# One transfer per tail, a new written order, and q of one batch transposed by DMA

## The chip, the cores and the metric

The kernel runs on one core of a Trainium2 chip. The metric is device time in microseconds (us), as the median of the timed runs. The core has a matrix engine (PE; its weight loads are listed as PEld), a vector engine (DVE), an activation engine (ACT), a general engine (POOL) and a sync engine (SP), which here issues every DMA from one queue in order (SPq is its sequencer).

## The reference

Two blocks follow one another. The first is attention with pooled keys: q, k and v are (8 batches, 8 heads, 576 tokens, 64). k and v are averaged over groups of 8 tokens, so each head has 72 pooled keys and values, and

```python
scores = scale * np.matmul(q, k_p.transpose(0, 1, 3, 2))
attn = softmax(scores)
x = matmul(attn, v_p)            # (8, 8, 576, 64), then reshaped to (8, 576, 512)
```

The second is a mixture of four attention experts on x. A gate picks two of four experts for each token, with softmax weights w. Each expert projects x to q, k and v of 64 columns, does causal attention over the 576 tokens, and projects back to 512 columns with wo. The output, (8, 576, 512) in float32, is the sum of the two picked experts, weighted by w.

## The kernel before, in words

**Tiles.** A batch's 576 tokens are handled as 512 main tokens, in four chunks of 128, and 64 tail tokens. The tails of two batches (an even one and the odd one after it) are put together to 128 rows and go through a path of their own (`part_t`, run with the odd batch).

**Units.** The work is cut into named units such as `3:s2` (batch 3, scores of head pair 2). A unit is a Python generator: its first step mostly issues the PE work, the next steps copy the result out of PSUM on DVE or ACT, mask on POOL, or store. The string `ORDER` at the top lists every step of every unit, and the loop at the end of the kernel issues them in just that order; each engine keeps it (`keep_in_program_order`). So the order of every engine's queue, and of SP's DMAs, is written out by hand in `ORDER`. A wait at the head of a queue holds everything behind it.

The names that matter here, by batch `b`:

- `lq`, `lk`, `lv` load the main tokens of q, k, v as float32 (batch 0 in four pieces, batch 1 in two); `lqt`, `lkt`, `lvt` load the tails. `W:lq`, `W:lk`, `W:lv`, `W:lo` load the weights, `W:c0` to `W:c3`, `W:cv`, `W:co` cast them.
- `qc` casts q to bf16 (`qbf`), `ks` and `vs` add up pairs of tokens, `kt` and `vt` cast the tails of k and v.
- `q0` to `q3` transpose q, one head pair each: four PE transposes into `qT_ps`, then a DVE copy to `qT`.
- `kp` and `vp` pool k and v by matmuls with the mask tiles `pm` (main) and `pmt` (tail).
- `s0` to `s3`: scores into `sA_ps`, then the exponential on ACT into `etA`. `a0` to `a3`: times v into `oA_ps`, then normalised on DVE into `x_tm`.
- `x0` to `x3`: transposes of x on PE; in batches 6 and 7 the DMA queue does them (`xd0` to `xd3`).
- `p0` to `p3`, `v0`, `v2`: projections into `p_ps` and `v_ps`; `g1` to `g6`: the gate; `c..`: expert scores (`sB_ps`, `etB`, `etC`); `o0`, `o1`: expert attention times values (`oB_ps`); `t0`, `t1`: its transposes (by DMA in batches 4, 5, 6); `w`, `y`, `z`: the output projection (`y_ps`), its copy (`w` on ACT, `y` on DVE, `z` both) and the store.
- `qt`, `qx`, `sx`, `ax`, `xx`, `pt`, `vx`, `h0`, `h1`, `hd`, `ox`, `tx`, `w4`: the same for the tails of two batches. `w4` ends with `yt_ps`, a copy to `ofin` and the store; `7:w4` is the last unit of the kernel.
- `W:h0` to `W:h31`: fillers, two matmuls each of zeros into `idle_ps`, 31 of them ahead of the first projection and one near the end.

**What is allotted.** PSUM is shared by two pools: `ps1` (two tiles) and `ps2` (three). The raw float32 tiles have two buffers for each of q, k and v, `ofin` has four. Each DMA signals on one of eight semaphores in turn, and waits until the DMA eight places ahead of it has landed.

**q in the last batches.** q's row r of a group of four neighbouring tokens lies in `qbf[:, r]`. In batches 0 to 5 the transposes of r write runs of 32 elements into `qT_ps`, with gaps between them, and the copy is plain. In batches 6 and 7, whose x the DMA queue transposes, tokens must stand in their natural order; there the transposes write without gaps and the copy (`COPY_IN_ORDER`) puts tokens in order.

**Tails of k and v.** A tail is loaded by two DMAs: heads 0 to 3 into partitions 0 to 63, heads 4 to 7 into partitions 64 to 127. `pmt[0]` and `pmt[1]` are the pooling masks of the two halves.

Of the kernel before, what the change touches and what calls it, by code (L numbers as in the profile page):

```python
# [22 lines left out]
0:lk2 0:qc2a 1:q0 1:q1 0:qc0a W:h29 0:qc0d 1:q1 W:h1 0:lk0 W:h21 0:qc1d 0:qc1a 0:lk3 0:q0 0:lv0 W:h7
W:h3 0:qc3d 0:q0 0:ks2 0:q1 0:lk1 0:q1 0:lv2 W:h8 0:ks3 W:h19 W:h14 0:kp2 0:lvt 0:qc2d 0:lv3 0:ks0
0:q2 0:kp2 0:lv1 0:q2 1:kt W:h6 0:vs2 1:lq1 W:h2 0:kp3 0:ks1 W:h27 0:qc3a W:h18 0:q3 1:lk0 0:kp3
0:q3 0:kp1 0:s2 0:vs0 1:lk1 0:kp1 0:s1 0:vs3 0:vt 0:vs1 0:s3 0:kp0 W:h26 0:kp0 1:lv1 W:h15 0:vp 0:s1
0:s2 1:lvt W:h25 0:vp 1:lv0 W:h22 1:qc1a 0:s3 0:a2 1:qc1d 0:s0 W:h16 W:lk W:h24 0:a3 W:h5 0:lqt 0:a2
1:q2 1:ks0 W:h13 1:ks1 1:kp0 0:a3 1:q2 0:s0 0:a1 1:kp0 0:a0 W:h4 1:kp1 W:h28 1:q3 0:a0 1:kp1 0:a1
W:h17 1:s0 0:x0 1:s0 1:s2 1:q3 1:s3 0:x0 1:s1 W:lq W:lv 1:s2 1:lqt 1:vs1 0:x1 1:s3 2:lq W:h10 W:h9
0:x3 0:x1 1:vt W:h0 W:c1 0:x2 1:vs0 2:lkt 0:x3 2:lk W:c3 0:x2 1:vp 1:vp 0:p1 1:a0 1:a2 1:a2 1:s1  # L30
0:p1 W:c2 W:c0 0:p3 1:a1 1:qt 1:a0 2:qc 2:lv 1:a1 0:p3 0:p2 1:a3 W:cv 0:p0 0:p2 0:v2 0:p0 1:a3 2:kt
3:lqt 1:x2 0:v2 1:qx 0:c10 0:c10 0:c2 0:v0 2:lvt 1:qx 1:x3 1:x2 0:v0 0:c2 1:x0 1:x3 3:lk 0:c11 1:x0
1:sx 1:x1 1:x1 0:c11 0:c11 0:c00 0:c00 0:g1 0:g2 2:q3 2:q3 2:q0 1:sx 1:v2 0:c2 3:lvt 2:q2 0:c01 2:ks
2:lqt 0:c10 3:lkt 1:ax 2:q2 2:q1 2:q0 1:ax 1:p1 1:p1 1:v0 0:c01 2:kp 2:q1 1:v2 1:p2 2:vs 2:kp 0:g3
2:vt 1:v0 1:xx 2:s2 3:lq 1:xx 1:p2 2:s0 2:s1 1:vx 0:g4 2:s2 2:s1 1:vx 2:s0 3:lv 1:g1 2:s3 0:g5 1:g2
2:vp 0:o1 2:vp 2:s3 1:pt 2:a2 0:g6 3:ks 1:pt 3:kt 2:a0 1:p3 4:lq 3:qt 0:c01 0:o1 2:a3 2:a2 0:c00
1:p0 1:g3 2:a0 1:p3 2:a3 2:a1 1:c11 3:qc 3:kp 1:p0 4:lk 3:qx 3:vt 2:a1 1:hd 3:qx 1:c11 1:h0 1:hd
1:c2 3:kp 2:x2 2:x1 1:h0 2:x2 4:lkt 0:o0 2:x1 2:x3 4:lv 4:lvt 2:x0 1:c10 1:c2 1:g4 0:o0 3:sx 2:x3
1:c00 3:q1 2:x0 1:c2 1:c10 1:c00 3:q3 1:h1 3:q1 3:q3 3:q2 3:q0 2:v2 3:vs 1:h1 3:q2 1:c11 4:qc 3:q0
5:lq 0:t0 1:g5 0:t1 2:v0 2:v2 3:sx 3:s3 3:s1 0:t1 3:vp 0:t0 3:s3 2:p1 6:lvt 1:hd 4:ks 3:s1 2:p1 2:v0  # L40
3:s2 4:kt 1:c10 3:s0 3:vp 3:s2 3:a3 2:p0 3:a3 4:q2 3:a1 3:ax 4:q2 3:s0 4:q1 1:c01 2:p0 4:q3 4:q1
2:p3 1:c01 2:p3 5:lqt 2:c01 3:a1 4:q3 4:q0 3:ax 2:c01 3:a0 1:c00 4:q0 4:kp 4:kp 3:a2 3:a0 3:a2 2:p2
3:xx 2:p2 6:lkt 1:g6 4:s2 3:xx 4:s0 4:s0 5:lkt 4:s2 1:ox 3:x3 2:g1 1:c01 4:vt 1:o0 2:c00 4:s1 1:ox
3:x3 3:x1 4:vs 2:g2 2:c00 5:qc 4:vp 3:x1 4:s1 3:pt 4:s3 2:c11 3:pt 4:vp 1:o0 3:x0 3:x2 1:o1 2:c01
3:x0 W:lo 3:x2 5:q2 4:lqt 4:s3 2:c00 5:lk 2:c11 3:p3 5:q2 5:lvt 5:q3 1:o1 5:lv 2:c2 3:p3 2:c10 5:q1
4:a3 5:kt 2:c2 5:q3 2:c10 3:p1 4:a0 5:q1 3:p1 W:co 4:a3 3:p2 3:vx 4:a0 6:lqt 4:a1 3:p2 3:vx 3:v0
4:a1 7:lqt 3:v0 0:w0 2:g3 3:hd 6:lq 3:c10 2:c11 1:t1 4:a2 5:qt 2:g4 5:ks 0:w0 3:p0 1:t1 5:q0 4:a2
3:c10 3:hd 5:q0 5:vt 3:p0 3:h0 2:c2 3:c11 5:qx 5:kp 3:c11 3:v2 5:kp 5:qx 2:g5 0:w3 3:v2 3:h0 2:g6
4:x1 4:x1 5:s3 0:w3 3:g1 5:s1 4:x2 5:vs 1:t0 7:lkt 5:s3 2:c10 2:o0 6:lk 4:x2 0:w2 1:t0 4:x0 6:qc
2:o0 5:sx 5:s1 3:c2 3:c10 6:vt 0:w2 5:sx 5:s0 5:s0 7:kt 6:lv 3:c11 3:g2 4:x0 4:x3 5:vp 4:x3 3:c2  # L50
5:vp 3:hd 2:o1 4:p1 3:c2 2:o1 0:w1 4:p1 6:kt 5:s2 3:h1 0:w1 6:q3 6:q0 5:ax 6:q3 4:p0 6:q0 2:t0 3:h1
6:ks 5:ax 5:s2 3:g3 2:t0 0:w3 7:lvt 4:v2 2:t1 4:p0 6:q1 5:a2 3:g4 2:t1 7:qt 6:vs 5:a0 6:q1 5:a0 1:w3
4:p3 5:a1 1:w3 4:p3 5:a2 4:v2 4:p2 7:lq 5:xx 3:c00 3:c01 4:p2 5:a1 0:w2 6:kp 5:a3 3:c00 7:lk 5:xx
3:c01 6:kp 3:g5 3:g6 7:ks 0:w0 5:pt 6:q2 6:s3 5:a3 4:c01 6:q2 4:c00 5:pt 1:tx 1:tx 6:vp 5:x0 6:s3
4:v0 4:c00 5:x0 6:vp 2:w1 4:c01 4:v0 5:x3 6:s0 4:c2 2:w1 5:x1 5:x3 6:s1 5:x1 0:w1 6:s0 7:qc 6:s1
7:lv 2:w0 5:x2 3:o1 6:a0 5:x2 3:c01 2:w0 1:w4 3:c00 3:o1 5:p3 1:w4 4:c2 7:kp 6:a0 7:kp 4:g1 4:c10
4:c11 6:s2 5:p3 7:vs 4:c11 4:c10 7:q3 1:w4 3:ox 6:s2 7:q3 7:q2 5:v0 4:c10 3:ox 2:w1 6:a3 5:vx 7:q2
5:v0 2:w2 5:vx 6:a2 6:a1 6:a3 6:a2 1:w0 2:w2 1:w0 4:g2 2:w0 5:p2 2:w3 5:p2 5:hd 7:s3 6:a1 1:w0 7:q1
2:w3 5:hd 7:q1 4:c00 7:vt 4:c2 5:hd 5:v2 4:c11 4:g3 1:w2 3:t1 5:h1 7:s3 7:s1 1:w2 5:h1 7:s1 6:xd2
5:v2 2:w3 3:t1 7:vp 5:g1 5:p1 6:xd3 7:s2 4:g4 2:w2 7:vp 5:c10 5:p1 7:a3 7:s2 7:a3 7:q0 7:q0 4:g5  # L60
5:p0 3:o0 5:g2 4:c01 3:o0 7:qx 6:xd0 5:p0 4:o0 1:w1 5:c10 5:c2 7:s0 4:g6 7:qx 6:xd1 1:w1 3:t0 7:s0
6:p3 5:g3 3:t0 3:tx 3:tx 6:v2 6:p3 6:p0 5:c2 7:a1 1:w1 4:o0 7:a0 3:w4 6:v2 4:t0 7:a1 6:p0 1:w2 3:w4
6:p1 7:a2 5:g4 7:a0 3:w2 3:w2 5:h0 7:a2 5:c10 5:g5 7:sx 4:o1 6:p1 4:o1 1:w3 3:y1 3:y1 6:p2 5:c11
7:sx 5:h0 5:g6 5:c01 7:xd0 7:xd1 5:c11 6:p2 5:c01 5:c00 5:ox 6:v0 4:t1 3:w2 3:w3 5:ox 3:w3 3:w0 6:v0
3:w0 5:c01 7:ax 7:v0 7:ax 7:v0 4:w2 5:c11 7:xx 7:xd3 6:c2 5:c2 7:xx 6:g1 5:c00 3:y1 4:w2 6:c00 5:o1
4:w3 6:c2 7:xd2 5:o1 7:vx 3:w3 7:v2 3:w4 6:g2 6:c2 4:w3 7:p2 6:c11 6:c00 6:c10 6:g3 5:c00 7:v2 7:p2
6:c11 7:vx 6:c01 5:t1 7:p3 4:y1 6:g4 7:p3 4:w3 7:g1 4:y1 6:c10 4:y1 5:o0 5:o0 7:g2 6:c01 6:c00 6:g5
4:y0 4:y0 5:t0 7:p0 6:c11 6:c10 6:o1 7:c11 7:p0 6:g6 7:c10 6:c01 7:g3 7:g4 6:o1 4:w2 7:p1 5:tx 6:o0
5:tx 6:o0 7:c10 7:p1 7:c10 3:w0 7:c11 5:w4 5:y1 6:t1 7:g5 7:c2 7:c01 5:w4 7:c2 7:c00 7:c11 5:y1 4:y0
7:g6 5:y2 7:c01 7:pt 7:c2 7:c01 7:pt 5:y2 6:t0 7:c00 5:y1 5:y0 5:y0 7:c00 7:o1 5:w3 7:o1 7:hd 6:y1  # L70
# [919 lines left out]
```

## Time and profile before

| | |
|---|---|
| median of the timed runs | 178.21 us (3 runs, 177.66 to 178.53) |
| the profiled execution | 176.43 us |
| its span | 174.7 us |
| granted TensorE clock, mean | 0.996 |
| HBM read, written | 30.42 MB, 9.44 MB |

The profile shows one execution. Its span runs from the first to the last instruction; the execution's own time is a little longer. Instructions are listed by the tile that they write and read (`qT_ps<-ident,qbf`), since all stand on one line of a helper. Matmuls overlap one another, so their durations don't add up to PE's time: what a further one costs is read from the length of a group of them. "Idle before" an instruction names the one whose end released it.

### The profile page before, as it was taken

What the parts mean: (1) busy time and instruction counts of PE and PEld (TensorE: products, weight loads), DVE (VectorE), ACT (ScalarE), POOL (GpSimd) and SP (SyncE); (2) the same over time, 40 slices, a digit from 0 to 9 for tenths busy, and PEclk for the clock granted to TensorE, in tenths of its full rate; (3) what the DMA queues carried; (4) which work ended last, traced back from release to release, by engine and by line L of the source; (5) the groups of instructions that cost most, each with busy time, mean ns of one, the idle gap of its engine ahead of it and who ended that gap; (6) DMA issues with size and microseconds to landing.
All of it is one profiled execution on the core that took longest, in us unless ns stands there. A gap on an engine that the chain in (4) does not pass through costs nothing.

```text
span 174.7 us, 5295 instructions
## 1 busy us (share of the span) xinstructions
PE 163.1 (93%) x2088; PEld 101.2 (58%) x2088; DVE 123.7 (71%) x354; ACT 125.0 (72%) x176; POOL 101.2 (58%) x227
## 2 busy tenths in 40 slices
...
GB/s 151 280 337 304 344 296 282 263 325 262 250 221 345 346 281 288 190 209 311 260 284 339 332 365 365 25 177 67 172 72 90 183 181 157 90 135 250 267 332 194
DMA packets 52968, 42.03 MB, mean 241 GB/s; under 512 B 21968, under 2 KB 48080, under 8 KB 52944
## 3 DMA queue, kind: packets, MB, share of 16 engines
...
HBM read 30.42 MB, written 9.44 MB: 228 GB/s over the span
## 4 chain that ended last, share of the span: by engine, by line
PE 72%; DMA 11%; ACT 8%; DVE 4%; SPq 1%; issue 1%; ACTq 0%; DVEq 0%
PE p_ps L133 15%; PE v_ps L133 7%; PE y_ps L133 6%; PE idle_ps L133 5%; PE sB_ps L133 5%; PE sA_ps L133 4%; PE oA_ps L133 4%; PE qT_ps L133 4%; PE oB_ps L133 4%; PE vp_ps L133 3%; DMA out_dram<-ofin 3%; DMA ktail<-in_k_dram 3%; PE xT_ps L133 3%; DMA kraw<-in_k_dram 3%; PE oBt_ps L133 3%; ACT etA L133 3%
## 5 line engine op out<-in xcount | busy, mean ns | idle before, releaser
L133 ACT ACTIVATE etA<-sA_ps 72x1024 bf16<-72x1024 f32 x32 | 31.4, 1018 | 12.7 <-PE sA_ps L133 12.6
L133 ACT ACTIVATE etB<-sB_ps 128x1024 bf16<-128x1024 f32 x32 | 32.3, 1027 | 3.0 <-PE sB_ps L133 2.7
L133 PE MATMUL p_ps<-xT,wqk 128*128 128x512 bf16 x128 | 32.9, 379 | 0.1
L133 POOL TENSOR_SCALAR_AFFINE_SELECT etB<-etB 128x256 bf16<-128x256 bf16 x48 | 18.5, 407 | 12.0 <-ACT etB L133 11.8
L133 ACT CAST qk<-p_ps 128x512 bf16<-128x512 f32 x32 | 18.8, 587 | 9.2 <-PE p_ps L133 9.0
L133 DVE TENSOR_TENSOR x_tm<-oA_ps,rzA 128x512 bf16<-128x512 f32 x32 | 22.1, 691 | 1.1
L133 POOL TENSOR_TENSOR vsum<-vraw 128x512 bf16<-128x512 f32 (+2 forms) x18 | 18.4, 1043 | 7.5 <-DMA vraw<-in_v_dram 7.5
L133 PE MATMUL idle_ps<-idle 128*128 128x512 bf16 x64 | 19.6, 418 | 1.9 <-DVE idle L160 1.2
L133 PEld LDWEIGHTS <-wqk 128*128 128x128 bf16 x192 | 15.0, 97 | 10.3 <-issue 0.9
L133 POOL TENSOR_TENSOR ksum<-kraw 128x512 bf16<-128x512 f32 (+1 forms) x16 | 17.8, 1134 | 4.8 <-DMA kraw<-in_k_dram 4.6
L133 PE MATMUL y_ps<-wo_t,oT 128*128 128x512 bf16 x64 | 18.4, 379 | 1.0 <-DMA oT<-o_sc 0.7
L133 DVE COPY qT<-qT_ps 128x512 bf16<-128x512 bf16 x32 | 15.2, 486 | 5.8 <-PE qT_ps L133 5.5
L133 ACT COPY ofin<-y_ps 128x512 f32<-128x512 f32 x20 | 11.7, 586 | 10.0 <-PE y_ps L133 6.8
L133 PE MATMUL v_ps<-wvg,xT 128*128 128x260 bf16 x128 | 17.0, 274 | 0.0
L133 PE MATMUL qT_ps<-ident,qbf 128*128 128x128 bf16 x128 | 11.9, 220 | 2.1 <-DVE qbf L133 1.4
L133 PE MATMUL sB_ps<-qk 64*128 64x256 bf16 (+3 forms) x128 | 13.6, 299 | 0.0
L133 DVE COPY xT<-xT_ps 128x512 bf16<-128x512 bf16 x24 | 9.7, 419 | 4.6 <-PE xT_ps L133 4.5
L133 PEld LDWEIGHTS <-xT 128*128 128x128 bf16 x128 | 11.6, 97 | 2.4 <-DVE x_tt L133 0.4
L133 POOL CAST qbf<-qraw 128x2048 bf16<-128x2048 f32 x6 | 11.3, 1889 | 2.8 <-PE sB_ps L133 2.4
L133 PEld LDWEIGHTS <-etA 72*128 72x128 bf16 x256 | 10.6, 97 | 3.9 <-issue 1.0
L133 PEld LDWEIGHTS <-qbf 128*128 128x128 bf16 x128 | 8.3, 97 | 7.4 <-issue 2.7
L133 PEld LDWEIGHTS <-etB 128*128 128x128 bf16 x256 | 11.4, 97 | 1.7 <-POOL etB L133 0.5
...
## 6 DMA issues: line engine op xcount, KB each, us to landing
out_dram<-ofin SPq DMA_DIRECT2D x28, 256.0 KB, 2.7
...
qraw<-in_q_dram SPq DMA_DIRECT2D x4, 256.0 KB, 4.7
...
kraw<-in_k_dram SPq DMA_DIRECT2D x4, 256.0 KB, 4.8
```

The source lines that it names most:

```text
L133: return tc.keep_in_program_order(fn(*args, **kwargs))
```

## The change

1. **Tails of k and v.** One DMA loads a tail. Partition 2t + half then holds token t, heads 0 to 3 (half 0) or 4 to 7 (half 1). The masks `pmt` are made anew: one mask over pairs of partitions on POOL, multiplied on DVE by the parity of the partition.
2. **Stores of tails.** `w4` stores the tails of both batches by one DMA. In `7:w4` the copy to `ofin` is split: the first 256 columns on ACT, the others on DVE.
3. **q of batch 7.** Four DMA transposes (`7:qd0` to `7:qd3`), one for each r, write `qT`; the units `7:q0` to `7:q3`, with 16 PE transposes and four DVE copies, are gone. The transposed tile keeps its four r apart, and the scores matmul of batch 7 reads it so and writes each result to the place of its token: every fourth float32 of `sA_ps`.
4. **Order.** `ORDER` is written anew throughout.

The diff without `ORDER`, of which three places follow:

```diff
+Q_BY_DMA = (7,)
-COPY_IN_ORDER = (6, 7)
+COPY_IN_ORDER = (6,)
+SCORES_IN_ORDER = (7,)
...
     pm = pooling("pm", 0, POOLW // NR)
-    pmt = [pooling("pmt0", MAIN, POOLW), pooling("pmt1", MAIN - 64, POOLW)]
-    nc.gpsimd.memset(pmt[1][0:64, :], 0.0)
+    rows = pooling("pmr", 2 * MAIN, 2 * POOLW)
+    parity = const.tile([128, 2, 1], BF16, name="parity")
+    nc.vector.tensor_reduce(
+        out=parity[:, :, 0], in_=ident[:, :].rearrange("p (i half) -> p half i", half=2),
+        axis=AX_X, op=MAXOP,
+    )
+    pmt = []
+    for half in range(2):
+        t = const.tile([128, 128], BF16, name=f"pmt{half}")
+        nc.vector.tensor_tensor(
+            out=t[:], in0=rows[:], in1=parity[:, half, :].to_broadcast([128, 128]), op=MULT
+        )
+        pmt.append(t)
...
-            for half in range(2):
-                sp.dma_start(
-                    out=t[half * 64 : half * 64 + 64, :].rearrange("p (h d) -> p h d", h=4),
-                    in_=srcs[nm][b, half * 4 : half * 4 + 4, MAIN:S, :].rearrange("h t d -> t h d"),
-                )
+            sp.dma_start(
+                out=t[:].rearrange("p (h d) -> p h d", h=4),
+                in_=srcs[nm][b, :, MAIN:S, :].rearrange("h t d -> t h d"),
+            )
...
+        def q_dma(r):
+            if "qD" not in st:
+                st["qD"] = apool.tile([128, NR, NHP, 128], BF16, name="qT", tag="qT")
+            sp.dma_start_transpose(
+                out=st["qD"][:, r, :, :], in_=st["q"][:, r, :, :].rearrange("p h d -> p (h d)")
+            )
...
+                to, rhs = ps[:, hh, :], st["qT"][r0 : r0 + D, hp, :] if "qT" in st else None
+                if b in SCORES_IN_ORDER:
+                    to = to.rearrange("s (p r) -> s r p", r=NR)
+                    rhs = (
+                        st["qD"][r0 : r0 + D, :, hp, :] if "qD" in st
+                        else rhs.rearrange("d (r p) -> d r p", r=NR)
+                    )
                 pe.matmul(
-                    out=ps[:, hh, :], lhsT=kp[r0 : r0 + D, hp, :],
-                    rhs=st["qT"][r0 : r0 + D, hp, :], start=True, stop=True,
+                    out=to, lhsT=kp[r0 : r0 + D, hp, :], rhs=rhs, start=True, stop=True,
                 )
...
+        if b in Q_BY_DMA:
+            names.update({f"qd{r}": lambda r=r: q_dma(r) for r in range(NR)})
...
             t = ofp.tile([128, DM], FP32, name="ofin", tag="ofin")
-            copy(out=t[:], in_=ps[:])
-            yield
-            for i, b_ in enumerate(both):
-                store(out[b_, MAIN:S, :], t[i * TAIL : (i + 1) * TAIL, :])
+            if b < B - 1:
+                copy(out=t[:], in_=ps[:])
+            else:
+                for half, eng in ((slice(0, DM // 2), act.copy), (slice(DM // 2, DM), dve.tensor_copy)):
+                    eng(out=t[:, half], in_=ps[:, half])
+            yield
+            store(out[b - 1 : b + 1, MAIN:S, :], t[:])
```

Of the order: the head of the list, before and after, and the place of the transposes of q in the new list, up to the first scores that need them.

```diff
-0:lq0 W:h12 1:lq0 0:lkt W:h20 0:lq2 0:lq3 W:h30 0:kt 1:qc0a W:h23 1:lkt W:h11 1:qc0d 0:lq1 1:q0
+W:h21 W:h1 0:lq0 0:lk0 0:qc0d 0:lq3 W:h24 W:h15 0:qc3a 0:lq1 W:h18 0:qc0a 0:qc1d 0:lkt W:h2 W:h14
...
+4:c01 2:w1 5:x1 3:c01 5:x1 6:s0 2:w1 6:s1 6:s0 7:lv 1:tx 5:x0 4:c2 1:tx 5:x2 3:g5 7:qd0 6:s1 5:x0
+5:x2 6:a3 7:ks 2:w0 0:w1 7:qd2 5:p3 3:g6 3:o1 4:c2 7:qd1 2:w1 6:s2 3:c00 6:a3 2:w0 4:c11 5:vx 4:c01
+4:g1 3:o1 5:p3 7:qd3 7:kp 4:c10 6:s2 4:c11 4:c10 4:c2 5:hd 5:vx 3:ox 7:qt 2:w0 7:kp 5:hd 6:a1 1:w4
+1:w4 6:a0 3:ox 4:g2 6:a2 6:a1 4:g3 6:a2 1:w4 7:vs 1:w0 6:a0 5:hd 1:w0 4:g4 2:w3 5:v2 2:w2 2:w3 2:w2
+5:p2 5:p2 7:s3 2:w3 5:v2 5:h1 7:s2 7:s3 7:vp 7:vp 1:w2 5:h1 5:v0 1:w2 5:p1 7:qx 7:s2 4:c11 5:v0 0:w3
...
```

More of the change, by code (lines that the diff above doesn't have):

```diff
@@ L21 @@
 ORDER = """
-0:lq0 W:h12 1:lq0 0:lkt W:h20 0:lq2 0:lq3 W:h30 0:kt 1:qc0a W:h23 1:lkt W:h11 1:qc0d 0:lq1 1:q0
[L23 to L70, printed above, removed]
@@ L71 @@
-7:o0 5:w3 6:w0 5:y2 5:y0 6:y1 7:hd 7:o0 7:h1 7:t1 6:w0 7:h0 7:t0 7:t1 7:t0 7:h1 7:hd 5:w3 5:w4 6:y3
-6:w0 6:y1 6:y3 6:y3 7:h0 7:z2 7:ox 6:w2 7:z2 7:z0 7:ox 7:tx 6:w2 7:tx 6:w2 W:h31 7:w4 7:z0 7:w4 7:w4
+W:h21 W:h1 0:lq0 0:lk0 0:qc0d 0:lq3 W:h24 W:h15 0:qc3a 0:lq1 W:h18 0:qc0a 0:qc1d 0:lkt W:h2 W:h14
+0:lk1 0:kt W:h30 W:h11 0:lq2 0:ks0 0:qc2a 1:lq1 0:lv2 0:lk3 W:h12 W:h9 0:kp0 0:lv1 0:lk2 W:h3 0:kp0
+0:qc2d 0:qc1a 0:lv0 W:h29 0:lvt 0:lv3 0:q0 W:h17 W:h13 0:qc3d 0:q0 1:lq0 0:ks1 0:q1 W:h10 1:lkt
@@ new lines @@
+W:h28 W:h26 1:lk1 0:ks3 1:lk0 0:vs0 1:lv1 0:q1 W:h5 0:vt 0:q3 0:q2 0:vs1 0:q2 0:kp1 0:q3 0:vs2 1:lv0
+0:s0 0:kp1 0:s1 0:ks2 1:ks1 1:kt W:h19 0:kp3 0:kp3 W:h4 0:kp2 1:qc1a 0:vs3 1:qc1d 1:ks0 1:lqt 0:s1
+0:vp 0:kp2 W:h23 0:s3 1:qc0d 1:qc0a 1:vs0 W:h20 1:q3 0:vp W:lq 1:lvt 1:q0 0:s0 W:lk 0:s2 0:lqt 1:vt
+1:q0 0:s3 1:q3 W:lv 0:a3 0:a1 2:lq 0:a1 W:h6 1:q2 W:h25 1:q2 0:s2 1:kp1 0:a2 W:h0 1:q1 0:a3 0:a0
+1:kp1 1:q1 0:a2 0:a0 W:h8 1:kp0 1:kp0 W:h7 1:s3 1:s3 0:x2 1:s2 1:s0 W:h22 1:vs1 2:lkt 2:lvt 2:lk
+1:s2 0:x3 0:x3 1:qt 1:s1 2:qc W:c0 1:s1 W:c2 0:x1 1:s0 0:x2 W:h16 0:x1 W:h27 0:x0 1:vp 0:x0 1:vp
@@ new lines @@
+W:c1 0:p2 1:a3 2:kt 0:p0 W:c3 0:p2 1:a2 2:lv 3:lk 1:a0 1:a3 1:a1 0:p0 0:p3 W:cv 1:a0 0:p3 1:a2 1:a1
+0:p1 1:qx 0:p1 0:c10 0:c11 1:x2 1:qx 1:x1 0:v2 3:lqt 1:x2 1:x1 1:x0 1:x3 0:c11 0:v0 0:v2 1:x3 1:sx
+1:x0 0:c10 0:v0 0:g1 2:lqt 1:sx 0:c11 2:q3 1:v2 2:q3 0:c10 3:lkt 1:p1 1:ax 2:q2 0:g2 1:v2 0:g3 0:g4
+0:c2 1:p1 1:ax 2:q0 0:g5 3:lvt 1:v0 2:ks 2:q2 3:lq 2:q0 2:q1 1:xx 0:c00 0:g6 0:c2 0:c01 2:q1 0:c2
+1:xx 0:c00 2:kp 2:vt 1:v0 2:kp 2:vs 3:lv 1:vx 0:o1 2:s2 3:ks 1:vx 0:c01 3:kt 1:p2 2:s2 2:s3 2:s1
+0:o1 2:s0 1:p2 2:vp 2:vp 1:g1 2:s1 1:p0 2:a2 2:s0 1:pt 2:a2 4:lq 2:a0 2:a1 2:s3 0:c00 2:a0 1:p0
@@ new lines @@
+0:c01 2:a3 1:pt 3:kp 2:a1 2:a3 3:qc 1:p3 1:p3 1:h0 0:o0 3:kp 0:o0 4:lkt 2:x3 1:h0 1:c11 2:x0 4:lk
+1:c11 1:c00 1:c10 3:qt 1:c11 1:c00 2:x0 2:x3 2:x2 2:x2 2:x1 1:c2 1:h1 4:lv 3:vs 1:c10 3:q3 2:x1 3:q2
+2:v0 1:c2 3:q2 4:lvt 3:qx 3:q3 2:v0 3:q0 1:h1 3:qx 3:q0 2:v2 1:g2 1:hd 1:hd 3:vt 3:q1 0:t1 2:v2 4:qc
+W:lo 4:kt 0:t1 3:q1 3:s3 3:sx 3:sx 2:g1 3:s0 0:t0 0:t0 3:vp 1:hd 6:lqt 3:s1 1:g3 3:s0 2:p1 3:vp 1:g4
+3:s3 4:q2 2:p1 4:q2 4:ks 3:ax 3:ax 3:a3 2:p3 3:a3 3:a0 5:lq 4:q0 3:s1 4:q0 3:s2 2:p3 3:a1 2:g2 3:a1
@@ new lines @@
+3:s2 4:q3 2:p0 4:q3 3:a0 1:c10 1:c01 2:p0 3:a2 4:vt 4:kp 2:p2 1:c01 1:c01 4:kp 1:g5 3:xx 2:c01 2:c00
+3:xx 2:p2 1:g6 1:c2 1:c00 4:q1 3:a2 1:ox 4:q1 3:x3 4:vs 4:s0 2:c01 4:s1 3:x3 1:ox 2:c00 4:s0 1:o0
+3:x2 2:g3 2:c00 5:qc 3:pt 4:s1 3:x2 3:pt 4:s2 5:lk W:co 4:s3 5:lvt 3:x0 4:s2 3:x1 5:lkt 1:o0 3:x0
+3:x1 4:lqt 1:o1 4:vp 1:o1 3:p3 4:vp 4:s3 2:c10 2:c11 2:g4 3:p3 5:q2 5:lv 4:a0 5:q2 2:c10 3:p2 3:p2
+4:a0 2:c2 5:kt 5:ks 2:c2 5:q3 2:c11 3:v0 5:q3 5:q1 3:p1 5:q1 3:p1 4:a3 1:t1 3:v0 2:c2 5:lqt 3:hd
+3:c11 2:c11 6:lkt 2:c10 3:hd 6:lq 0:w0 0:w0 1:t1 0:w0 3:vx 5:qt 4:a2 6:lv 4:a3 7:lkt 3:vx 5:vt 4:a1
@@ new lines @@
+4:a2 3:c11 7:lvt 2:g5 3:p0 3:p0 3:h0 3:c10 4:a1 3:hd 2:c01 5:q0 5:kp 5:q0 3:c10 3:h0 2:g6 5:vs 3:v2
+0:w3 0:w3 5:kp 4:x0 3:v2 5:s1 6:kt 5:s1 5:s3 1:t0 4:x0 5:qx 1:t0 5:qx 3:g1 5:s3 2:o0 3:g2 6:lk 4:x2
+6:qc 0:w2 7:lq 5:sx 6:lvt 4:x2 5:s0 6:vs 4:x3 2:o0 6:ks 0:w2 5:vp 5:s2 5:sx 4:x3 4:x1 5:vp 3:c11
+5:s0 2:o1 3:c10 0:w1 7:qc 5:s2 4:x1 5:a0 0:w1 2:o1 4:p1 6:q0 0:w2 3:c2 5:a0 4:p1 6:vt 3:c2 6:q0 3:h1
+2:t1 7:kt 6:q3 2:t1 3:h1 6:q3 5:ax 2:t0 5:a3 4:p0 2:t0 7:lk 4:p0 5:ax 5:a1 4:p3 5:a1 5:a3 5:xx 4:p3
@@ new lines @@
+4:v2 1:w3 5:xx 1:w3 4:v2 6:q1 7:vt 3:c01 3:c00 6:kp 3:c01 6:q1 6:kp 5:a2 4:p2 5:a2 6:q2 4:c01 3:g3
+6:q2 3:g4 3:c00 6:s3 7:lqt 4:p2 4:c00 3:c2 5:x3 5:pt 6:s3 4:c00 5:x3 6:vp 6:vp 5:pt 4:v0 4:v0 1:w3
+4:c01 2:w1 5:x1 3:c01 5:x1 6:s0 2:w1 6:s1 6:s0 7:lv 1:tx 5:x0 4:c2 1:tx 5:x2 3:g5 7:qd0 6:s1 5:x0
+5:x2 6:a3 7:ks 2:w0 0:w1 7:qd2 5:p3 3:g6 3:o1 4:c2 7:qd1 2:w1 6:s2 3:c00 6:a3 2:w0 4:c11 5:vx 4:c01
+4:g1 3:o1 5:p3 7:qd3 7:kp 4:c10 6:s2 4:c11 4:c10 4:c2 5:hd 5:vx 3:ox 7:qt 2:w0 7:kp 5:hd 6:a1 1:w4
@@ new lines @@
+1:w4 6:a0 3:ox 4:g2 6:a2 6:a1 4:g3 6:a2 1:w4 7:vs 1:w0 6:a0 5:hd 1:w0 4:g4 2:w3 5:v2 2:w2 2:w3 2:w2
+5:p2 5:p2 7:s3 2:w3 5:v2 5:h1 7:s2 7:s3 7:vp 7:vp 1:w2 5:h1 5:v0 1:w2 5:p1 7:qx 7:s2 4:c11 5:v0 0:w3
+7:s1 4:g5 7:qx 5:p1 5:c10 6:xd3 7:s1 3:t1 3:o0 5:p0 5:g1 3:t1 6:xd1 7:s0 6:xd0 3:tx 4:c00 5:c10 7:a1
+3:o0 6:xd2 5:p0 5:g2 7:a3 4:g6 1:w1 7:s0 3:tx 7:a1 3:w4 7:a3 7:a0 1:w1 2:w2 7:a2 7:a0 5:c10 6:p2
+5:g3 4:c10 5:g4 7:a2 6:v2 3:w4 5:g5 1:w0 4:o0 6:p1 6:p2 3:t0 6:v2 4:o0 7:sx 7:xd0 6:p1 7:sx 5:c11
```

10 lines of the change are left out of this document (added).

## The prediction

> **What bounds the kernel now.** I read the page first, then sums over stretches of the span, then single rows of the timeline, the waits and the transfers.
>
> ```profile
> span 174.7 us, 5295 instructions
> PE 163.1 (93%) x2088; PEld 101.2 (58%) x2088; DVE 123.7 (71%) x354; ACT 125.0 (72%) x176; POOL 101.2 (58%) x227
> PE 72%; DMA 11%; ACT 8%; DVE 4%; SPq 1%; issue 1%; ACTq 0%; DVEq 0%
> ```
>
> PE is busy for 93% of the span, and the chain of work that ended last runs through PE for 72% of it. The next engines have 71% and 72%. So a step is worth what it takes off PE, or what it moves at the two ends, where PE waits. The stretches (span of the stretch; then PE, PEld, DVE, ACT, POOL busy with their counts; granted clock, DMA share, GB/s) show where that is:
>
> ```profile
> 0.00:5.00 5.00, 3.77 (x9) 1.35 (x10) 3.54 (x6) 1.28 (x1) 4.38 (x18) 1.00 0.57 172
> 5.00:10.00 5.00, 3.31 (x22) 1.50 (x21) 1.39 (x4) 1.33 (x3) 1.99 (x16) 1.00 1.06 278
> 0.00:30.00 30.00, 25.74 (x182) 11.94 (x183) 18.83 (x52) 11.22 (x16) 13.58 (x45) 1.00 1.02 286
> 30.00:170.00 140.00, 137.19 (x1907) 89.26 (x1905) 104.41 (x303) 113.21 (x160) 87.67 (x182) 1.00 0.85 232
> 155.00:160.00 5.00, 4.32 (x57) 2.63 (x56) 3.08 (x8) 4.23 (x6) 2.40 (x8) 1.00 0.78 192
> ...
> 0.00:30.00 30.00, 19.02 (x62) 1.00 1.02 286
> ```
>
> The last row counts the filler matmuls (idle_ps) alone. There are three stages. In the first 30 us PE has 25.74 - 19.02 = 6.7 us of real work; it waits for loads, and the DMA engines are full (1.02). From 30 to 170 us PE stands visibly idle for 140 - 137.19 = 2.8 us only, the largest piece (0.7 us) at 155 to 160. After 170 us the last tail tile is copied and stored. The granted clock is 1.00 in all of them.
>
> **The change part by part.** The sum is made against the profiled execution: 174.7 us span, 176.43 us in all, so 1.7 us lie around the span. The median of the timed runs is 178.21 us, 1.8 us above that execution; I carry the difference over to the median.
>
> *q of batch 7.*
>
> ```profile
> L133 PE MATMUL qT_ps<-ident,qbf x128: 216/219/230, 7.1 to 126.9; 128*128 128x128 bf16 x128
> 115.06 0.40 PE L133 MATMUL qT_ps<-ident,qbf 128*128 128x128 bf16 x4
> 115.50 0.69 DVE L133 COPY qT<-qT_ps 128x512 bf16<-128x512 bf16 x1
> L133 PE MATMUL oT_ps<-ident,o_sc 128*128 128x128 bf16 x40 | 3.7, 220 | 0.2 <-DVE o_sc L133 0.2
> ```
>
> Four transposes end 0.40 us after the first begins, and one takes 0.22, so each further one costs PE (0.40 - 0.22) / 3 = 0.06 us. Sixteen go: -0.96 us, in the stage that PE bounds. Four DVE copies of 0.69 us go too (2.8 us), off the path, since DVE is busy 71%: I count nothing; the gain could be some tenths where a PE step waited for DVE. Four transposes come to SP's queue. They stand behind 7:lv, the last load, and are interleaved with stores; no load is behind them.
>
> ```profile
> xT<-x_tm SPq DMA_TRANSPOSE x8, 3.3
> 101.79 0.52 SPq L133 DMA_DIRECT2D vraw<-in_v_dram  x1
> 113.65 7.17 SPq L133 DMA_DIRECT2D out_dram<-ofin  x5
> 113.70 0.23 PE L133 MATMUL kpT_ps<-pm,ksum 128*128 128x72 bf16 x2
> 121.18 0.38 PE L133 MATMUL sA_ps<-qT,kp 64*128 64x512 bf16 x2
> ```
>
> Between that last load at 101.8 us and 113.65 us SP issued nothing. A transpose of the same size landed 3.3 us after its issue. In the new order 7:qd3, the last of the four, stands right ahead of 7:kp, and 7:s3 is the first to need it; before, 7:kp began at 113.70 us and 7:s3 at 121.18 (the sA_ps row), 7.5 us later. So I cost the transposes at nothing: 7.5 - 3.3 = 4.2 us of cover. If that is gone, PE stands at 7:s3 with everything behind it (a rival below).
>
> *Scores that write in steps.*
>
> ```profile
> 16.75 0.60 PE L133 MATMUL sA_ps<-qT,kp 64*128 64x512 bf16 x4 [0.24 <-DVE kp L133]
> L133 PE MATMUL sA_ps<-qT,kp x64: 372/386/387, 16.1 to 130.1; 64*128 64x512 bf16 x64
> ```
>
> The two heads of a unit run side by side: a second pair adds 0.60 - 0.39 = 0.21 us. In batch 7 each result goes to every fourth fp32 element. No row shows such a write. The nearest: in batches 0 to 5 the qT_ps transposes write runs of 32 elements with gaps, and their median is 219 ns, as the gapless oT_ps's 220. That would make the step free; but a run of one is not a run of 32. So the bounds are 0 and, at four times the time, 4 x 3 x 0.21 = +2.5 us; I take half of a doubling, 4 x 0.21 / 2 = +0.43, near the free end because the nearest row is free. The Trainium skill, "PSUM — Partial Sum Buffer", section Specifications, speaks against the change: PSUM's cachelines are 8 bytes, and any non-contiguous pattern "slows matmuls significantly". The trace's runs of 32 elements show no such slowing; that they are longer than a cacheline would fit both. If the rule meant a doubling here, the sum would be 0.43 us worse; it gives no figure.
>
> *The end.*
>
> ```profile
> 169.75 0.69 DVE L133 COPY kraw<-y_ps 128x512 f32<-128x512 f32 x1 [0.21 <-ACT kraw L133]
> 170.28 0.59 ACT L133 COPY ofin<-yt_ps 128x512 f32<-128x512 f32 x1 [0.56 <-PE yt_ps L133]
> 170.90 1.11 SPq L133 DMA_DIRECT2D out_dram<-ofin  x2
> L133 ACT CAST qbf<-qraw 128x256 bf16<-128x256 f32 x4 | 1.4, 402 | 2.3 <-DMA qraw<-in_q_dram 2.3
> L133 DVE CAST vat<-vt_ps 128x256 bf16<-128x256 f32 x4 | 1.7, 416 | 0.0
> out_dram<-ofin SPq DMA_DIRECT2D x28, 256.0 KB, 2.7
> out_dram<-ofin SPq DMA_DIRECT2D x8, 128.0 KB, 2.4
> ```
>
> The last copy (0.59 us) is split between ACT and DVE, which looks like a saving. But both halves read the same PSUM tile, and the first row shows what the framework does then: DVE's half of kraw waits for ACT's half. In the changed program DVE's half of ofin waits for ACT as well. So it costs 0.40 + 0.42 + about 0.05 of handover = 0.87, not 0.59: +0.28. Two stores of 0.55 us issue each become one: -0.55. The one is larger: 2.7 - 2.4 = +0.3. Sum 0, bounds -0.55 (landing no later) and +0.3.
>
> *One transfer for a tail, and the start.*
>
> ```profile
> 1.79 1.41 SPq L133 DMA_DIRECT2D ktail<-in_k_dram  x2
> 4.40 1.27 SPq L133 DMA_DIRECT2D ktail<-in_k_dram  x2
> 30.96 1.02 PE L133 MATMUL p_ps<-xT,wqk 128*128 128x512 bf16 x4
> ```
>
> Sixteen loads go, and four of the eight tail stores (one is counted above). Each costs SP some 0.6 us, which matters only where the DMA engines aren't full: the first 5 us (share 0.57). Two pairs lie there, so SP gains (1.41 + 1.27) / 2 = 1.34 us, and the stream of loads can move up by that much. What it brings is read at the first projection, 30.96 us: both orders put the same PE steps ahead of it (31 filler units, batch 0's attention up to x, batch 1's q, kp, s and vp), and it waits for the last weights and for ACT's exponentials. The weights stand behind some 0.1 MB more in the new order, at 286 GB/s 0.4 us. So between -1.34 and +0.4; I take -0.6. The two mask tiles move from POOL to three short DVE operations ahead of the first ksum, and DVE waits there for data anyway: nothing.
>
> *The new order.* Between 30 and 170 us it can at best take away the 2.8 us of idle PE, at worst add as much again. By the rows' durations, fewer steps of the new order stand tight behind what they need, but what queues on ACT and DVE isn't in such a count: 0, bounds -2.8 and +2.8. The joint stores of tails 1, 3 and 5 lie here, off the path.
>
> Sum: -0.96 + 0.43 + 0 - 0.6 + 0 = -1.1 us. The profiled execution would come to 175.3, its span to 173.6, the median to 178.21 - 1.1 = 177.1 us.
>
> **The rivals.** About 0.5%, or 0.9 us, is what a measurement of this kernel can tell from no change.
>
> *The order closes the gaps.*
>
> ```profile
> PE y_ps L133 <- DMA oT<-o_sc: 0.7, 1, 0.7
> ```
>
> The longest late wait is that of y_ps for a transposed oT. If the new order starts those early enough, up to 2.8 us more go: 174.3 to 176.2 us. For it: the gaps are few. Against it: every re-planned order has some of its own.
>
> *The stepped write costs in full.* By the skill's page above, and as mechanism here: PE holds each pair longer. Doubled, 177.1 + 0.43 = 177.5, no change; at four times 177.1 + 2.1 = 179.2, slower. Against it: the rows of 32-element runs.
>
> *The transposed q comes late (slower).*
>
> ```profile
> SPq L133 <- ACT ofin L133: 21.2, 6, 11.3
> ```
>
> SP runs its queue in order and once waited 11.3 us for an ACT copy ahead of a store. In the new order the store of 2:w1 stands between 7:qd1 and 7:qd3. If it holds SP for more than the 4.2 us of cover, 7:s3 waits, and PE with it; 3 us beyond that give 177.1 + 3 = 180.1. Against it: that copy's place is some PE steps ahead of the store.
>
> *The new order brings waits of its own (slower).* As much idle PE again: 177.1 + 2.8 = 179.9.
>
> **How the numbers follow.** My forecast, 176.4 to 177.9, has 0.42 (0.30 of it faster by over 0.5%, 0.12 within it); gaps closed 0.16 (faster); stepped write 0.16 (half within 0.5%, half slower); late q 0.12 and new waits 0.14 (slower). So faster 0.46, within 0.5% 0.20, slower 0.34. The range, 174.6 to 180.2, leaves out the far ends of the gap and wait cases. Both signs hold much of the chance; the likeliest case's own range is 176.4 to 177.9.
>
> **What would show it.** In the changed profile: no qT_ps row after some 120 us and 112 of them in all; sA_ps of batch 7 with a pair still near 0.4 us (right) or 0.6 and more (stepped write dear); 7:s3 without a wait for a transpose; the first p_ps near 30.4 us; DVE's half of the last copy behind ACT's; PE from 30 to 170 us with about 2.8 us of gaps. More than 4 us of gaps there, or a first projection after 31.5 us, would prove the forecast wrong.

## The result, and the profile after

| | before | after |
|---|---|---|
| median of the timed runs | 178.03 us (4 runs, 177.66 to 178.53) | 196.2 us (4 runs, 195.35 to 197.85) |
| the profiled execution | 176.43 us | 195.35 us |
| its span | 174.7 us | 193.6 us |
| granted TensorE clock, mean | 0.996 | 0.946 |

The changed kernel takes 1.103 times as long, with a 95% interval of 1.0948 to 1.1111. Medians here and below are of all runs of a kernel, and ratios with their intervals are of its fast runs alone, those within 1.5% of its fastest: the 0.9872 of joint_by_token below is that of six of its ten runs (median 175.54 us), while the median of all ten is 176.19. From the changed kernel's page: the span, PE's row, the granted clock and the DMA share in 40 slices, and the chain of work that ended last, by engine and by line.

```profile
span 193.6 us, 5250 instructions
PE 167.1 (86%) x2072; PEld 102.4 (53%) x2072; DVE 122.2 (63%) x354; ACT 125.8 (65%) x176; POOL 100.7 (52%) x222
PEclk9999999999999999999999999979998799985975
DMA  5999999999999999939997952970298366854630
PE 64%; DMA 19%; DVE 4%; SPq 3%; ACT 3%; issue 2%; POOL 1%; DVEq 0%; ACTq 0%
DMA out_dram<-ofin 12%; PE p_ps L135 12%; DMA kraw<-in_k_dram 7%; PE v_ps L135 7%; PE y_ps L135 5%; PE sB_ps L135 5%; PE oB_ps L135 4%; PE oA_ps L135 4%; PE xT_ps L135 4%; PE sA_ps L135 3%; SPq L135 3%; PE qT_ps L135 3%; PE oBt_ps L135 3%; PE vp_ps L135 2%; PE kpT_ps L135 2%
```

PE has fallen from 93% to 86%, and at the head of the chain's lines stands a transfer: the store of `ofin`. The chain itself, its pieces that are stores (start, length), and the waits for them (us in total, times, longest):

```profile
116.94 7.75 DMA out_dram<-ofin
138.52 8.27 DMA out_dram<-ofin
167.39 7.74 DMA out_dram<-ofin
```

```profile
ACT ofin L135 <- DMA out_dram<-ofin: 11.9, 2, 6.4
DVE ofin L135 <- DMA out_dram<-ofin: 9.2, 2, 5.5
PE oT_ps L135 <- DVE ofin L135: 5.3, 1, 5.3
PE vp_ps L135 <- ACT ofin L135: 4.4, 1, 4.4
PE y_ps L135 <- DVE ofin L135: 3.0, 1, 3.0
```

Three stores take some 8 us each where the median of all is 2.6. They are the joint stores of tails 1, 3 and 5. `ofin` has four buffers: four copies later, a copy on ACT or DVE needs the buffer that such a store still reads, and waits at the head of its engine's queue. PSUM tiles are then not emptied, and PE stands: 4.4 + 3.0 + 5.3 = 12.7 us. The fourth joint store is the last of the kernel:

```profile
184.03 0.37 ACT L135 COPY ofin<-yt_ps 128x256 f32<-128x256 f32 x1 [0.81 <-PE yt_ps L135]
184.43 0.42 DVE L135 COPY ofin<-yt_ps 128x256 f32<-128x256 f32 x1 [0.49 <-ACT ofin L135]
184.88 0.53 SPq L135 DMA_DIRECT2D out_dram<-ofin  x1
```

From its issue to the end of the span it is 193.6 - 184.88 = 8.7 us; before, from the issue of the last stores, 174.7 - 170.90 = 3.8. That is 4.9 more, and 12.7 + 4.9 = 17.6 of the 18.9 us by which the span grew. The stretches show the standing time, and why the store is long:

```profile
120.00:125.00 5.00, 1.01 (x20) 0.34 (x16) 0.00 (x0) 0.21 (x1) 0.00 (x0) 1.00 1.19 165
125.00:130.00 5.00, 4.57 (x22) 2.46 (x22) 1.54 (x4) 4.26 (x7) 0.00 (x0) 0.66 0.72 192
145.00:150.00 5.00, 2.35 (x50) 2.11 (x50) 1.73 (x9) 1.93 (x4) 0.69 (x3) 0.89 0.82 134
170.00:175.00 5.00, 0.69 (x11) 0.29 (x8) 0.00 (x0) 0.41 (x2) 0.76 (x2) 0.78 0.49 137
175.00:180.00 5.00, 4.00 (x46) 2.38 (x46) 3.12 (x7) 2.52 (x3) 0.00 (x0) 0.54 0.45 165
188.00:192.00 4.00, 0.00 (x0) 0.00 (x0) 0.00 (x0) 0.00 (x0) 0.00 (x0) 0.50 0.13 46
```

In the last row nothing is left but that store, and the DMA share is 0.13: of 16 DMA engines two are at work (2/16 = 0.125). Its destination, `out[b-1:b+1, MAIN:S, :]`, has two batches as its outermost axis. The Trainium skill, "DMA: Bandwidth & Descriptors", section "Rules for kernel authors", says just this: the slowest axis of the access patterns sets the number of engines, and an outermost axis of c < 16 "confines the whole DMA to at most c engines". The trace agrees: c is 2, and the share is that of 2 engines. A further cost stands in the clock column: in the stretches in which PE resumes, at 125, 145 and 175 us, the granted clock is 0.66, 0.89 and 0.54, where every stretch of before from 0 to 170 us was at 1.00. What this costs by itself was not separated from the stalls.

### The profile page after: what moved, and what is told of

It reads as the page before. It is cut to its first block, busy times and chain, and to the rows that moved or that the text cites. A ratio compares the mean times of both kernels' runs of the same rounds, so it can differ in the third digit from the quotient of the medians.

```text
span 193.6 us, 5250 instructions
## 1 busy us (share of the span) xinstructions
PE 167.1 (86%) x2072; PEld 102.4 (53%) x2072; DVE 122.2 (63%) x354; ACT 125.8 (65%) x176; POOL 100.7 (52%) x222
## 4 chain that ended last, share of the span: by engine, by line
PE 64%; DMA 19%; DVE 4%; SPq 3%; ACT 3%; issue 2%; POOL 1%; DVEq 0%; ACTq 0%
DMA out_dram<-ofin 12%; PE p_ps L135 12%; DMA kraw<-in_k_dram 7%; PE v_ps L135 7%; PE y_ps L135 5%; PE sB_ps L135 5%; PE oB_ps L135 4%; PE oA_ps L135 4%; PE xT_ps L135 4%; PE sA_ps L135 3%; SPq L135 3%; PE qT_ps L135 3%; PE oBt_ps L135 3%; PE vp_ps L135 2%; PE kpT_ps L135 2%
## 5 line engine op out<-in xcount | busy, mean ns | idle before, releaser
L135 PE MATMUL y_ps<-wo_t,oT 128*128 128x512 bf16 x64 | 19.9, 411 | 3.0 <-DVE ofin L135 3.0
L135 DVE COPY qT<-qT_ps 128x512 bf16<-128x512 bf16 x28 | 12.5, 457 | 6.6 <-PE qT_ps L135 6.5
L135 PE MATMUL sB_ps<-qk 64*128 64x128 bf16 (+3 forms) x128 | 14.1, 309 | 0.0
L135 PEld LDWEIGHTS <-xT 128*128 128x128 bf16 x128 | 12.3, 99 | 3.2 <-issue 0.6
L135 DVE COPY ofin<-y_ps 128x512 f32<-128x512 f32 x8 | 5.5, 690 | 12.0 <-DMA out_dram<-ofin 9.2
L135 PE MATMUL oB_ps<-vaug,etB 128*128 128x65 bf16 x256 | 12.4, 194 | 0.0
L135 PE MATMUL sA_ps<-qT,kp 64*128 64x512 bf16 x64 | 12.1, 410 | 0.0
L135 DVE CAST vp<-vp_ps 72x512 bf16<-72x512 f32 x8 | 5.5, 688 | 10.4 <-PE vp_ps L135 10.4
```

Source lines behind the costliest of these rows:

```text
L135: return tc.keep_in_program_order(fn(*args, **kwargs))
```

## The experiments

Three theories were on the table. A: the joint store, on two engines, is the loss. B: the new order, or the transposes of q, make stalls of their own. C: a store of 256 KB to two places is slow as one transfer. All times are medians; "before" beside them was timed on the same chip.

**Two tail stores again.**

```diff
-            store(out[b - 1 : b + 1, MAIN:S, :], t[:])
+            for i, b_ in enumerate(both):
+                store(out[b_, MAIN:S, :], t[i * TAIL : (i + 1) * TAIL, :])
```

> The changed kernel with the tail stores as before, one per batch. Theory A (the joint store, whose outer dimension is 2, runs on two DMA engines and holds what queues behind it): the four stalls of 3 to 8 us go; span 175 to 177, median 176 to 179 us, granted clock back near 0.99. Theory B (the new order with q by DMA makes the stalls, the stores only stand where they show): median stays above 190 us.

179.43 us against 177.03: 1.0125 (1.005 to 1.0201). So 0.09 of the 0.103 are the joint store's. But the median lies 0.4 us above what theory A expected, and what is left is still slower than before, not faster.

**The joint store alone, in the kernel before.**

```diff
-            for i, b_ in enumerate(both):
-                store(out[b_, MAIN:S, :], t[i * TAIL : (i + 1) * TAIL, :])
+            store(out[b - 1 : b + 1, MAIN:S, :], t[:])
```

> The kernel before with the joint tail store alone. Theory A: three or four stalls appear at the tail stores and the last store lands some 8 us after its issue instead of 2.4: median 188 to 198 us. Theory B: within 2 us of before, 176 to 180 us.

191.33 us, 1.072 (1.0618 to 1.0823). The old order suffers as well; the stores in its chain:

```profile
113.82 7.90 DMA out_dram<-ofin
149.59 8.71 DMA out_dram<-ofin
170.00 7.66 DMA out_dram<-ofin
```

**The joint store for the last pair only**, two stores for the other three (one run).

```diff
-            store(out[b - 1 : b + 1, MAIN:S, :], t[:])
+            if b == B - 1:
+                store(out[b - 1 : b + 1, MAIN:S, :], t[:])
+                return
+            for i, b_ in enumerate(both):
+                store(out[b_, MAIN:S, :], t[i * TAIL : (i + 1) * TAIL, :])
```

> The changed kernel with two stores for the first three pairs of tails and the joint one for the last pair. Theory A: no stall before the end, and the last store lands 7 to 8 us after its issue: 5 to 6 us above the kernel with two stores throughout, span 180 to 183 us. Theory B: stalls as in the changed kernel, span above 190 us.

183.42 us: one joint store at the end is worth 183.42 - 179.43 = 4.0 us by this one run, near the 4.9 read above and less than the 5 to 6 that I expected.

**The joint store cut into two by columns** (one run): two DMAs of half the bytes, each with the outermost axis of 2.

```diff
-            store(out[b - 1 : b + 1, MAIN:S, :], t[:])
+            for c in (slice(0, DM // 2), slice(DM // 2, DM)):
+                store(out[b - 1 : b + 1, MAIN:S, c], t[:, c])
```

> The changed kernel with each joint tail store cut in two by columns: two DMAs of 128 KB, as many and as large as before, but each with an outer dimension of 2 (its rows are 1 KB pieces). Theory A: each still runs on two engines; the pair lands in 8 us or more, span above 188 us. Theory C (one transfer of 256 KB is what is slow, two of 128 KB are not): span 175 to 178 us.

195.59 us: no gain, and C falls. The chain shows the second half of each pair, which still takes 7 us:

```profile
118.41 7.13 DMA out_dram<-ofin
140.16 7.22 DMA out_dram<-ofin
167.93 7.17 DMA out_dram<-ofin
```

This doesn't say that half the bytes take as long. The first half of the first pair was issued at 117.67 us, and the pair ended at 118.41 + 7.13 = 125.54, 7.9 us later: the two halves share the same engines (the DMA share with only the last pair under way, 188 to 191 us, is 0.13 again), and the pair takes as long as the one store did (7.75 us). What one half alone would take was not run.

**One joint store, walked token by token.** The copy to `oTt` interleaves the two batches, so the destination can be seen with 64 tokens outermost.

```diff
-            dve.tensor_copy(out=st["oT"][:], in_=ps[:])
+            dve.tensor_copy(
+                out=st["oT"][:].rearrange("p e (t i) -> p e t i", i=2),
+                in_=ps[:].rearrange("p e (i t) -> p e t i", i=2),
+            )
...
-            store(out[b - 1 : b + 1, MAIN:S, :], t[:])
+            store(out[b - 1 : b + 1, MAIN:S, :].rearrange("b t d -> t b d"), t[:])
```

> The changed kernel with its joint tail store kept as one DMA, but walked token by token: the copy to oTt interleaves the two batches, so row 2t + i of ofin is token t of batch i, and the destination is seen as (64 tokens, 2 batches, 512). The bytes and the packets of 2048 bytes are the same. If a store is spread over DMA engines by the outermost axis of its destination (64 here, 2 in the changed kernel), it uses all engines, lands in some 2.5 to 3 us instead of 7.7 to 8.3, and the time falls from 196 to about 179.4, that of the kernel with two stores; 178.8 if the store that is saved counts. If the joining of two batches by itself is slow, it stays at 194 to 197.

176.19 us, 0.9872 (0.9831 to 0.9914): the same bytes, one DMA, and 20 us less than the changed kernel. That settles A. It is also 3 us better than two stores, more than I expected; what may lie behind it stands in the next step.

**What still held up the kernel with two stores.** Its stretch of 140 to 155 us, below that of before; then its waits; then what SP issued in that stretch, and the chain through it.

```profile
140.00:155.00 15.00, 14.67 (x191) 9.55 (x188) 9.93 (x36) 11.54 (x19) 8.44 (x29) 1.00 0.56 151
```

```profile
140.00:155.00 15.00, 11.22 (x143) 7.45 (x144) 5.50 (x19) 9.70 (x14) 5.27 (x18) 0.89 0.48 145
```

```profile
ACT ofin L135 <- DMA out_dram<-ofin: 6.3, 3, 3.8
PE y_ps L135 <- ACT ofin L135: 2.4, 1, 2.4
```

```profile
138.82 1.27 SPq L135 DMA_TRANSPOSE xT<-x_tm  x1
140.20 1.20 SPq L135 DMA_TRANSPOSE oT<-o_sc  x1
141.44 1.26 SPq L135 DMA_TRANSPOSE xT<-x_tm  x1
142.81 1.21 SPq L135 DMA_TRANSPOSE oT<-o_sc  x1
144.06 6.20 SPq L135 DMA_DIRECT2D out_dram<-ofin  x5
```

```profile
144.06 4.21 DMA out_dram<-ofin
148.35 0.59 ACT ofin L135
148.99 0.60 PE y_ps L135 x2
```

SP issues four transposes one after the other, 1.2 us and more each, and behind them five stores. The store issued at 144.06 lands at 148.27; only then can ACT's copy begin, and PE's y_ps after it. Before, stores stood between the transposes of this stretch (at 140.45 and 142.32 us). PE has 11.22 us of work in these 15, where before it had 14.67; this is the 181.2 us run, whose first projection had already come 1.2 us later than before's, so not all of it is the queue's. Every store that SP needn't issue shortens this queue. That this is why one joint store beats two is argued, not shown: no run tests it by itself, and in the old order one joint store gained nothing (177.56 us, below). So theory B, with its mechanism: the copies wait for room in `ofin`. Next, the room was taken out of the question:

```diff
-            t = ofp.tile([128, DM], FP32, name="ofin", tag="ofin")
+            if b < 3:
+                t = ofp.tile([128, DM], FP32, name="ofin", tag="ofin")[:]
+            else:
+                nm = "qraw" if b % 2 else "vraw"
+                if "y" not in st:
+                    st["y"] = rawp.tile([128, H, NR * D], FP32, name=nm, tag=nm)
+                t = st["y"][:, 2 * c : 2 * c + 2, :].rearrange("p h n -> p (h n)")
```

> The changed kernel with two tail stores, and with room of its own for each main output tile of batches 3 to 6: it lies in raw tiles of q or v, which are free by then, and no copy waits for the store of an older one. In the kernel with two stores, copies to ofin waited 6.3 us (ACT) and 0.8 us (DVE) for stores, and PE stood for 2.5 us at 146 to 149 us and 0.9 at 166.7. If the new order's stores, queued behind transposes on SP, are what keeps it 2.4 us above the kernel before, those waits go and the time falls to 176.5 to 178. If the stepped write of the scores, or the DMA transposes, are the cause, or the next wait is as late, it stays within 0.6 of 179.4.

174.83 us, 0.9857 (0.9818 to 0.9896): 4.6 us less than with shared room, and faster than before. So B is shown for the rest, as far as the room goes: the waits for it are what kept this kernel above the one before. SP still issues transposes ahead of the stores here; that queue costs where a copy waits for room behind it.

**The step of batch 7's scores moved from the write to the read.**

```diff
-                    to = to.rearrange("s (p r) -> s r p", r=NR)
-                    rhs = (
-                        st["qD"][r0 : r0 + D, :, hp, :] if "qD" in st
+                    rhs = (
+                        st["qD"][r0 : r0 + D, :, hp, :].rearrange("d r p -> d p r") if "qD" in st
```

> The changed kernel with two tail stores; batch 7's scores write one run of 512 float32 again, and the matmul instead reads its moving operand in steps (token by token over the four r of the transposed tile, 1024 bytes apart in SBUF). If the step costs only where PSUM is written, the sA_ps matmuls of batch 7 go back from 0.60 to about 0.39 us a pair member, PE saves 4 x 0.21 = 0.85 us, and the time is 178.5 to 178.9 (179.4 if those units lie beside other waits). If a stepped read of SBUF is as slow as the stepped write, the matmuls stay at 0.6 us and the time at 179.4.

180.16 us, 1.0146 (1.0079 to 1.0213): no gain. The eight matmuls of batch 7 before, after and here (busy us, mean ns of one):

```profile
L133 PE MATMUL sA_ps<-qT,kp 64*128 64x512 bf16 x8 | 1.5, 380 | 0.0
```

```profile
L135 PE MATMUL sA_ps<-qT,kp 64*128 64x512 bf16 x8 | 2.4, 598 | 0.0
```

```profile
L135 PE MATMUL sA_ps<-qT,kp 64*128 64x512 bf16 x8 | 4.1, 1019 | 0.0
```

The stepped write adds 0.22 us a pair, the stepped read 0.64: I had named no price above the write's, and that was too low.

**q of batch 7 by PE again, in the kernel with two stores.** Part 3 undone: the `qd` steps go from the order, and the steps of `7:q0` to `7:q3` stand ahead of the scores that need them.

```diff
-Q_BY_DMA = (7,)
-COPY_IN_ORDER = (6,)
-SCORES_IN_ORDER = (7,)
+Q_BY_DMA = ()
+COPY_IN_ORDER = (6, 7)
+SCORES_IN_ORDER = ()
```

> The changed kernel with two tail stores, and part 3 undone: q of batch 7 is transposed on PE (16 transposes, four copies on DVE that put tokens in order), placed in the new order between the units where the kernel before has them, and the scores write one run. If the new order alone keeps the kernel with two stores above the one before, this gives 179.0 to 180 (it gives back 0.96 us of transposes and saves 0.85 us of stepped write). If the q transposes on the DMA queue hold up stores and loads (they add four entries to SP's queue at 103 to 111 us) it gives 177 to 178.

179.84 us, 1.0124 (1.0082 to 1.0166), as with the transposes. So the transposes of q aren't what kept the kernel with two stores above the one before: this is what I expected for the order alone. What part 3 is worth couldn't be told with the waits for stores in the way; it was asked again below.

**Both cures.** The edits of joint_by_token and two_own_room together, in the changed kernel:

> The changed kernel with the joint store walked token by token and with room of its own for the main output tiles of batches 3 to 6: both cures at once. If stores that land or are issued late, and the copies that wait for their room, are all that kept the new order back, this is the fastest so far: two_own_room was at 174.8, and four store issues of some 0.55 us less on SP give 174.0 to 174.8. If a wait that neither cure touches is next, it stays at 174.8 to 175.6.

173.65 us, 0.9799 (0.9766 to 0.9831): the fastest here, 2% below before and a little below what I expected. Its span, the same stretch, and the waits for stores that are left:

```profile
span 171.9 us, 5209 instructions
140.00:155.00 15.00, 14.39 (x198) 9.33 (x197) 9.58 (x32) 12.57 (x19) 7.18 (x24) 1.00 0.65 196
ACT ofin L135 <- DMA out_dram<-ofin: 1.1, 1, 1.1
168.62 0.55 SPq L135 DMA_DIRECT2D out_dram<-ofin  x1
```

PE's work in it is back from 11.22 to 14.39 us, and from the last joint store to the end it is 171.9 - 168.62 = 3.3 us, not 8.7.

**The same with q by PE.** The edit of two_q_by_pe in joint_own_room:

> The same with q of batch 7 transposed on PE again and scores that write one run: part 3 by itself, with no waits for stores that could hide it. By the sum of the pieces (16 transposes of 0.06 us are 0.96 more, four pairs of plain writes 0.85 us less) it is within 0.4 us of joint_own_room. If the four DMA transposes still hold up SP's queue, or the four copies off DVE don't matter and the stepped write does, it is 0.6 to 0.9 us faster; if the copies on DVE lie on the path, it is up to 1.8 us slower (four of 0.46 us).

175.74 us, 0.9902 (0.9871 to 0.9932), 2.1 us above joint_own_room: the transposes of q by DMA bring more than their pieces said, and more than the 1.8 that I gave as the most, with 0.46 us for a copy where those of batch 7 take 0.69. PE waits for DVE's copies of q (the first two rows), and a transposed x that is issued late comes into the chain (the third, start and length):

```profile
114.26 0.69 DVE L133 COPY qT<-qT_ps 128x512 bf16<-128x512 bf16 x1
115.00 0.23 PE L133 MATMUL kpT_ps<-pm,ksum 128*128 128x72 bf16 x2 [0.78 <-DVE qT L133]
```

```profile
141.72 4.08 DMA xT<-x_tm
```

Here the steps were put into an order written without them; an order planned for them might lose less. That wasn't tried.

**The kernel before with the joint store by token, and with room of its own**, one edit in each of two kernels.

> The kernel before with the joint store alone, walked token by token (with the destination's outermost axis of 2 this took it from 178 to 191.3). If the store's shape was all, it is 176.8 to 178: within 0.6 of the kernel before, or faster by up to 0.55 us for the store issue that is saved at the end. If part of the loss of the joint store lay in what waits for it as one, it is 179 or more.

177.56 us, 1.001 (0.9985 to 1.0034): within what can't be told from no change, where the joint store with the two batches outermost stood at 1.072. The store's shape was all.

> The kernel before, with two tail stores, and room of its own for the main output tiles of batches 3 to 6. Its copies waited only 0.7 us (ACT) and 0.7 us (DVE) for stores, so it should gain 0 to 0.8 us: 176.8 to 177.8. Then what is left of the 3.2 us by which two_own_room (174.8) beats the kernel before (178.0) belongs to the new order and the transposes of q, not to the room. If it falls to 175 or below, the room is worth the same to both orders, and the new order by itself gives nothing.

175.63 us, 0.9899 (0.9851 to 0.9947). A miss: two waits of 0.7 us led me to 0.8 at most, and it brought 1.9. So the room serves the old order too, though less than the new (4.6).

Two of these times, from the same chip, say what the new order is worth. joint_own_q_by_pe has the new order, the single loads and the joint store, but q by PE: 175.74 us. The kernel before with the same room has none of these: 175.63. With the room equal, the new order, the loads and the store show no gain together, and what joint_own_room has over both kernels (2.0 to 2.1 us) came with part 3. The caution above holds: the order was written for the transposes on the DMA queue.

## Why the prediction was wrong

I forecast 177.1 us; it is 196.2. The step that failed is the landing of the joint store, which I priced by its bytes. It comes twice, in the first two points:

- **The end: the step that failed.** The order of the copies was read rightly: DVE's half begins at 184.43, behind ACT's. The store was issued in 0.53 us for two of 0.55. But its landing was taken from the stores of 256 KB, 2.7 us, as if bytes set it. Those have 128 tokens outermost, this one has 2 batches. The term "+0.3" was some 5 us (4.9 by the traces, 4.0 by last_joint).
- **"The joint stores of tails 1, 3 and 5 lie here, off the path."** The same step a second time, and the larger part: 12.7 us of standing PE. PE was busy for 132.39 of the 140 us between 30 and 170 us; 7.6 us of gaps are more than the 4 that I had named as a sign against me. I asked what a later landing costs at the end, but not who needs the buffer next: a store off the path holds one of four `ofin` buffers, and that chain leads over ACT and DVE to PE. No rival priced a store that lands late.
- **The new order.** I set 0, with +2.8 as the bound and as a rival. With two stores PE has 11.22 - 14.67 = -3.45 us of work in 140 to 155 us, so the rival came true, at about its price: 2.4 us by the medians. It did so as long as the outputs shared four buffers; with room of their own the order shows, together with the loads and the store, neither loss nor gain (175.74 against 175.63 us). The place of its cause, what queues on ACT and DVE, I had named as what my count couldn't see.
- **Stepped write.** Bounds 0 and +2.5, taken +0.43; it is almost exactly the doubling of the added time (0.84), (0.598 - 0.380) x 4 = +0.87 us. The rule of the Trainium skill, "PSUM — Partial Sum Buffer", section Specifications, held for this write: the trace agrees, with 598 ns for 380. For the transposes' runs of 32 elements no run here shows it (219 ns, against 220 without gaps), and that nearest row misled me.
- **q on the DMA queue.** The transposes were not late. They landed 5.3 us after issue by the median, not 3.3; but the last was issued at 109.53 us and 7:s3 began at 119.74, so 119.74 - 109.53 - 5.3 = 4.9 us of cover were left. The gain of 0.96 us was too small: in joint_own_q_by_pe part 3 is worth 2.1 us together with its own stepped write. There DVE's copies of q, counted at nothing, lie on the path: PE waits 0.78 and 0.54 us for two of them, in a profiled run of 177.23 us. Another 1.4 us is the late x, so how much of the 2.1 is the copies' stays open.
- **The start.** The first projection stood at 30.33 us where I expected 30.4 instead of 30.96:

```profile
30.33 1.02 PE L135 MATMUL p_ps<-xT,wqk 128*128 128x512 bf16 x4
```

```profile
32.13 1.02 PE L135 MATMUL p_ps<-xT,wqk 128*128 128x512 bf16 x4
```

  But the second row is two_stores, whose program is the same up to there. One execution can't confirm 0.6 us at the start. The traces of all runs together speak against it: ten kernels with the new start reached it at 30.23 to 32.13 us, 30.80 in the middle, and the four with the old one at 30.28, 30.96, 31.13 and 31.34. That is 0.2 us between the medians, within the spread, so the -0.6 isn't seen. No run tried the single loads by themselves.

With the store's shape mended, the kernel comes out about where the sum aimed: joint_by_token is 1.3% below before, where I expected 0.6%. That is luck in part, for the parts aren't those of the sum: q brings more than its 0.96 us, the start's 0.6 isn't seen, the stepped write costs twice its 0.43, and the waits for room, which the sum didn't have, are still in it.
